# Accumulating Strassen products onto copies in PSUM, with two more weight pairs of the first block pair in Strassen form

## The chip, the cores and the metric

The kernel runs on one core of one Trainium2 chip. The metric is device microseconds (us) of one execution. Five engines take part: PE (TensorE, the matrix products), ACT (ScalarE), DVE (VectorE), POOL (GpSimd) and SP (SyncE, which issues most DMAs). Matrix products land in PSUM, which has eight banks of 128 x 512 float32; ACT and DVE read and write it.

## The reference

```python
# chunked attention: 8 batches, 8 heads, 576 tokens, chunks of 64, head_dim 64
scores = scale * np.matmul(q_c, k_c.transpose(0, 1, 2, 4, 3))
attn = softmax(scores)
x = np.matmul(attn, v_c)          # laid out as 4608 tokens x 512
# a gated layer on it: w_in 512 x 2048, w_out 2048 x 512
h = x @ w_in
g = h * np.clip(h + 3.0, 0.0, 6.0) / 6.0
out = (g @ w_out).astype(np.float32)
```

## The kernel before, in words

**Tiles.** The 4608 tokens are nine blocks of 512. An attention unit such as 21 is half of the heads of block 2. The hidden size of 2048 is 16 tiles of 128, the contraction over 512 is four slices. Every operand of the large products is split into a high and a low float32r part, and `passes` (lines 471 to 475) issues three matmuls of 128x512 for one slice: high by high, high by low, low by high.

**Block 0** is computed plainly: steps `a`, `b` (first product), `c` (second product). **The other eight blocks** go in four pairs, s = 0 to 3. A pair's two blocks and the hidden tiles p and p+8 form a 2x2 problem, for p = 0 to 7, which `first_product` (line 1040) does in Strassen form: seven products `f1` to `f7` in the order `ORDER_A`, each two slices by three matmuls, so 42 matmuls for a p. In plain form a p takes four tiles of four slices by three matmuls, so 48. In the pair s = 0 the first `NPL` = 4 of the p are done plainly, since their weight sums are not made yet; they are made later from weight tiles (`sum_steps`, line 558; the list `LATER`).

**How the seven products are put together.** Before, product 1, 5, 6 and 7 each get a fresh bank. ACT copies product 1 to SBUF (`p1`, line 1090). DVE adds: `u2` = product 6 + `p1`, `u4` = product 5 + `u2`, `s7` = product 7 + `u4`, and after products 3 and 4 `s3` and `s4` (all through the helper at line 1032). Product 2 accumulates onto product 1's bank after `p1`, product 3 onto that of 5 after `u4`, product 4 onto that of 7 after `s7`. Each of the four results goes through `add_relu_gate` (line 902): ACT writes relu into a tile `r` (line 907), DVE multiplies it with the bank into a `wb` tile (line 910). `second_product` (line 1153) has the same form on the eight weight tiles of w_out, in units of two banks e = 0, 1, and sends sums out of line 1165.

**What sets the order.** Every step is added to `Schedule` with an engine, a cost, the steps it comes after and a due time. `order` (line 102) works the latest start of each step back from the due times and lists the steps engine by engine; each engine then runs its list in order, and an engine that waits holds up all that is behind it. PSUM banks are taken in rings through `take`: ring h has two banks, ring o four. The weight sums for the Strassen form go through `whole` (a load of 256 KB by two DMAs at line 575 if the weight tile is in `KEPT`, else DVE adds at 578), `comb` (DVE, lines 583 and 586), `top` (ACT, 591), `less` (DVE, 594) and `send` (DMAs at 599).

The lines on which product 3's wait rests:

```python
j = {2: 1, 3: 5, 4: 7}.get(i, i)
if i == j:
    after += take_bank(i, name, [id_({1: "gate2.", 5: "gate3.", 7: "gate4.", 6: "gate7."}[i])])
else:
    after.append(id_({2: "p1.", 3: "u4.", 4: "s7."}[i]))
```

Of the kernel before, what the change touches and what calls it, by code (L numbers as in the profile page):

```python
# [18 lines left out]
P = 128  # L19
CH = 64  # L20
# [17 lines left out]
ORDER_B = (1, 5, 6, 7, 2, 4, 3)  # L38
# [20 lines left out]
KEPT = [f"a{i}" for i in range(8)] + ["b3", "b7"]  # L59
# [6 lines left out]
AFTER = {7: -14}  # L66
DUE = {'10': 13.5, '11': 15.25, '20': 16.5, '21': 21, '30': 28, '31': 34.25, '40': 37, '41': 37.5}
SUMS = (-8, 3.7, 2, 0.8)
# [5 lines left out]
TURNS = {1: [*range(NPL, NFP), *range(NPL)]}  # L74
# [3 lines left out]


class Schedule:  # L80
# [21 lines left out]
    def order(self):  # L102
# [47 lines left out]
def tile_kernel(ctx: ExitStack, tc: tile.TileContext, qk_in, v_in, weights, out):  # L150
# [85 lines left out]
    class Attention:  # L236
# [116 lines left out]
        def product(self, bank=None, part=(0, 1)):  # L353
            if part[0]:
                po = self.po
            elif bank:
                po = [bank().rearrange("p (a i t) -> p a i t", a=2, t=CH) for _ in HALF]
                self.src = [t.rearrange("p a i t -> p (a i) t") for t in po]
            else:
                t = self.out()  # L360
                po = self.po = [t[:, s].rearrange("p (a i t) -> p a i t", a=2, t=CH) for s in range(2)]
                self.src = t.rearrange("p s (k t) -> p s k t", t=CH)
            for a in part:
                for i in range(NB // 2):
# [29 lines left out]
    class First(Attention):  # L394
# [122 lines left out]
    def store(n, et, ps):  # L517
        if et % 2 == 0:
# [39 lines left out]
    def sum_steps(m, p):  # L558
# [12 lines left out]
        def whole():  # L571
            t["a"] = borrow(4 * (p % 2), F32)[:, :1024].rearrange("p (f t) -> p f t", f=2) if late else sp.tile([P, 2, 512], F32, name="a")
# [15 lines left out]
        def high():  # L588
            t["hl"] = parked[m, p] = borrow(4 * (p % 2) + 1, F32R).rearrange("p (f k l t) -> p f k l t", f=2, k=2, l=2) if late else hp.tile([P, 2, 2, 2, 256], F32R, name="hl")
# [11 lines left out]
        def send_own():  # L601
            for i, row, col in ((1, 0, 0), (2, 0, 1), (4, 1, 1)):
# [6 lines left out]
    GRAIN = [2] * NSUP  # L609
    turns = lambda s: TURNS.get(s, [*range(NFP)])  # L610
    parts = lambda t, n, g: [t[:, k:min(k + g, n)] for k in range(0, n, g)]
    stream = [t for s in range(NSUP) for t in [t for p in turns(s) for h in range(2) for t in parts(stream_a[p, h], 4 - h, GRAIN[s]) if s]
              + [t for i in ORDER_B for h in range(2) for t in parts(stream_b[i, turns(s)[4 * h] // 4], 4, GRAIN[s])]]
# [24 lines left out]
    def next_slot(s, name, until, stream=False):  # L638
# [10 lines left out]
        if len(work.rings[f"slot{k}"]) == 1:  # L649
            before = [f"f4.0.{2 * (k % 4) + 1}" if 2 * (k % 4) >= NPL else f"b{2 * NFT + 2 * k + 1}", *owns(k)]  # L650
# [37 lines left out]
    def first_x_steps():  # L688
# [19 lines left out]
        def high(i):  # L708
            ops[0][i] = w_tile(f"a{HELD[i]}", F32R)
            ACT.copy(out=ops[0][i][:, :, 0], in_=t(i))  # L710

        def lower(i):
            DVE.tensor_tensor(out=ops[0][i][:, :, 1], in0=t(i), in1=ops[0][i][:, :, 0].bitcast(F32), op=ALU.subtract)
# [10 lines left out]
        for i, last in ((5, "x0.s0"), (6, "x0.s1"), (7, "x0.s2"), (4, "x0.s3")):  # L724
            k = HELD[i]
            before = work.take(f"slot{k}", 1, f"x0.{i}h", [f"f{i}.0.{NFP - 1}"])
            assert not before
            work.add(f"x0.{i}h", "ACT", 1.05, [last, f"b{2 * NFT + 2 * k + 1}", *owns(k)], lambda i=i: high(i))
            work.add(f"x0.{i}l", "DVE", 1.22, [f"x0.{i}h"], lambda i=i: lower(i))

    def operand(s, i, ct):
        if s == 0 and i in (1, 2, 3):
            x = xs[{1: (1, 0), 2: (1, 1), 3: (2, 1)}[i]]
            return x[:, 0, ct], x[:, 1, ct]
        x = ops[s][i][:, ct]
# [20 lines left out]
    def attention(u, due, scores=(), less=(), keep=(), bank=None):  # L756
# [10 lines left out]
        if u in ROWS:  # L767
# [4 lines left out]
                  ["v" + u, *(["qk" + after, *[x for _ in HALF for x in work.take(*RINGS[bank], "product" + u, [made[u], *alike.get(u, [])])]] if after else [])]),  # L772
# [52 lines left out]
    PLACES = {"20": ("a", NFT), "21": ("a", NFT + 10), "30": ("f", 0, 4), "31": ("s", 0, 0), "40": ("s", 0, 2), "41": ("s", 0, 4)}  # L825
    AT = {1: (("f", 1, 4), ("f", 1, 7), ("s", 1, 2), ("s", 1, 4)), 2: (("f", 2, 3), ("f", 2, 6), ("s", 2, 1), ("s", 2, 4))}
# [28 lines left out]
    RINGS = {}  # L855
    bank_h, bank_o = lambda: ps_h.tile([P, NT], F32, name="h"), lambda: ps_o.tile([P, NT], F32, name="acc")
    RINGS.update({bank_h: ("h", 2), bank_o: ("o", 4)})
# [72 lines left out]
    for pos, (n, ft) in enumerate(mm):  # L930
        j = n * NFT + ft
        prev = mm[pos - 1][0] * NFT + mm[pos - 1][1]
        first, second, relu, gate, high, lower, sums, send, bank, under = tile_steps(n, ft)
# [3 lines left out]
        before = [] if apart and j % 2 else [f"b{prev}" if pos else None]  # L937
        work.add(f"a{j}", "PE", PART / 3 if apart else PART, [f"{'high' if apart else 'lower'}a{ft // 2}" if n == 0 else None, *before, "keep00" if apart else made[f"{n}0"], *work.take("o" if spare_bank(pos) else "h", 4 if spare_bank(pos) else 2, f"a{j}", [f"gate{j}"])], first, due=at)
# [18 lines left out]
        for et in range(NET):  # L957
# [3 lines left out]
            if j == 0:  # L961
                before += work.take("o", 4, name, [f"copy{et}"])
# [28 lines left out]
    for u in [*[u for u in range(NFP) if u not in AFTER], *range(NFP + NPL, 2 * NFP), *AFTER, *LATER]:  # L991
        m, p = 1 - u // NFP, u % NFP
        whole, combine, high, lower, send, send_own = sum_steps(m, p)
        due = SECOND + AFTER[u] if u in AFTER else STEPS + SUMS[0] + SUMS[1] * (u - 7) if u < NFP else STEPS + SUMS[2] + SUMS[3] * PART * 7 * (p - NPL) if p >= NPL else START[1] + LATE[0] + LATE[1] * p
# [4 lines left out]
        next_ = {0: ["ul0.7.1", "ul0.4.1"], 1: ["ul0.2.1", "ul0.3.1"], 2: [f"send{NFP}"], 3: [f"send{NFP + 1}"]}[p] if late else work.take("hl", 2, f"top{u}", [f"send{u}", *last])  # L999
# [11 lines left out]
    SLOT_OF = (2, 0, 5, 6, 4, 1, 3, 7)  # L1011
    FREED = (3, 5, 7, 2, 6, 4, 1, 0)

    bank = lambda i: ps_h.tile([P, NT], F32, name="h") if i in (6, 3) else ps_o.tile([P, NT], F32, name="acc")
    take_bank = lambda i, name, until: work.take("h", 2, name, until) if i in (6, 3) else work.take("o", 4, name, until)
# [24 lines left out]
    def first_product(s):  # L1040
# [5 lines left out]
        for at, p in enumerate(turns(s) if s else range(NPL, NFP), 0 if s else NPL):  # L1046
            t = {}
            more = lambda r, p=p: left(p + NFP * r) if s == 0 else [f"less{u}s" for u in LATER] if s == 1 and p < 2 else [f"send{u}" for u in LATER] if s == 1 and p < NPL else []
# [3 lines left out]
            for k, i in enumerate(ORDER_A):  # L1052
                name = id_(f"f{i}.")
                j = {2: 1, 3: 5, 4: 7}.get(i, i)
                feed, until = feeds[ceil(4) * (k // 4) + k % 4 // g] if s else (None if i in (1, 2, 4) else f"less{NFP + p}s", [])
                over = s and (k % 4 % g == g - 1 or k == 6)
                after = [before, feed, f"x{s}.{i}l" if s or i in HELD else None]
                if i == j:
                    after += take_bank(i, name, [id_({1: "gate2.", 5: "gate3.", 7: "gate4.", 6: "gate7."}[i])])
                else:  # L1060
                    after.append(id_({2: "p1.", 3: "u4.", 4: "s7."}[i]))

                def product(i=i, j=j, k=k, t=t, over=over, p=p):
                    w = ahead[0][:, k % 4 % g] if s else weight_of(p, i)
                    ps = t[j] if i != j else keep_tile(t, i, lambda: bank(i))
                    for ct in range(2):
                        o = slice(ct * P, ct * P + P)
                        passes(ps, w[:, 0, o], w[:, 1, o], *operand(s, i, ct), i == j and ct == 0, ct == 1, i != j)
# [3 lines left out]
                due = START[s] + PART * (7 * at + k)  # L1072
# [6 lines left out]
                def fresh(key, p=p):  # L1079
                    if s:  # L1080
# [216 lines left out]
```

## Time and profile before

| what | value |
|---|---|
| time, median of 3 runs | 765.35 us (765.1 to 765.86) |
| the profiled execution, span from first to last instruction | 764.3 us |
| what lies around the span, against the median | 1.05 us |
| instructions | 13998 |
| PE busy | 757.2 us, 99% of the span |
| DVE busy | 640.9 us, 84% |
| ACT busy | 451.2 us, 59% |
| DMA | 198.05 MB, 259 GB/s on average |

The page gives no time of the profiled execution other than its span, so a run's time is read as the span and 1.05 us around it. Busy time is summed over instructions; PE's matmuls overlap and their ends are modelled, so how far apart they start says more than how long they are busy. "[0.55 <-DVE u L1032]" behind a row means that the engine was idle for 0.55 us before it and that a DVE instruction of line 1032, which writes `u`, released it.

### The profile page before, as it was taken

The page shows a single profiled execution, that of the slowest core. Times are in us where ns is not written, and L with a number is a line of the kernel's source. Part 1 is how long each engine was busy: PE and PEld are TensorE (multiplying, and loading weights), DVE is VectorE, ACT ScalarE, POOL GpSimd, SP SyncE. Part 2 cuts the span into 40 slices and gives each one's busy share as a digit, 9 for nine tenths or more (in the row PEclk, how much of TensorE's full clock was granted, in tenths as well). Part 3 has the DMA queues.
Part 4 walks back from the last instruction along what each step waited for, and adds up shares of the span by engine and source line. Part 5 has one row for each costly group of instructions (what it writes and reads, how often), then busy time and mean ns, then how long its engine had stood idle before and what let it go on. Part 6 is the DMA issues. An engine that isn't in the chain of part 4 may idle for free.

```text
span 764.3 us, 13998 instructions
## 1 busy us (share of the span) xinstructions
PE 757.2 (99%) x5457; PEld 621.4 (81%) x5457; DVE 640.9 (84%) x805; ACT 451.2 (59%) x884; POOL 69.9 (9%) x74
## 2 busy tenths in 40 slices
PE   8999999999999999999999999999999999999998
PEld 5788788888888888788888888888888888888887
DVE  6989989898999999898999697689996667679751
ACT  6898967675768844356884444557853333355330
POOL 0000000000000010121200103201001123221010
PEclk9999999999999999999999999999999999999999
DMA  9999999959486898986667865757657666565572
GB/s 370 406 361 374 330 354 343 314 206 313 168 288 242 294 389 279 319 267 211 216 241 243 315 229 195 256 195 274 197 195 238 218 211 193 194 207 193 193 242 90
DMA packets 67442, 198.05 MB, mean 259 GB/s; under 512 B 7024, under 2 KB 19568, under 8 KB 63024
## 3 DMA queue, kind: packets, MB, share of 16 engines
q1 hardware_dynamic: 64752, 188.90, 71.9%
q0 software_dynamic: 2480, 8.13, 2.7%
q8 instruction: 43, 0.70, 0.4%
q14 instruction: 23, 0.19, 0.1%
q10 hardware_dynamic: 144, 0.13, 0.1%
HBM read 153.09 MB, written 44.04 MB: 258 GB/s over the span
## 4 chain that ended last, share of the span: by engine, by line
PE 85%; DMA 5%; DVE 5%; ACT 3%; issue 1%; SPq 0%; DVEq 0%; ACTq 0%
PE acc L473 21%; PE acc L474 20%; PE acc L475 20%; PE h L473 7%; PE h L474 7%; PE h L475 7%; DMA wb<-w_in_out 3%; PE two L263 2%; PE h L367 1%; DMA wb<-wa 1%; DMA xd<-qk_in 1%; ACT r L212 1%; ACT e L345 1%; ACT u L208 1%; DVE u L215 1%
## 5 line engine op out<-in xcount | busy, mean ns | idle before, releaser
L473 PE MATMUL acc<-wa,ws 128*128 128x512 f32 (+1 forms) x536 | 208.8, 390 | 0.5 <-DVE u L1032 0.5
L474 PE MATMUL acc<-wa,ws 128*128 128x512 f32 (+1 forms) x536 | 207.8, 388 | 0.0
L475 PE MATMUL acc<-wa,ws 128*128 128x512 f32 (+1 forms) x536 | 207.8, 388 | 0.0
L1140 ACT CAST wa<-wb 128x1024 fp32r<-128x1024 f32 x96 | 100.1, 1053 | 78.2 <-PE acc L475 49.1
L1144 DVE TENSOR_TENSOR wa<-wb,wa 128x1024 fp32r<-128x1024 f32 x96 | 119.0, 1257 | 17.3 <-ACT wa L1140 17.2
L473 PEld LDWEIGHTS acc<-wa,ws 128*128 128x128 f32 x536 | 100.6, 188 | 22.2 <-DVE u L1032 1.3
L475 PEld LDWEIGHTS acc<-wa,ws 128*128 128x128 f32 x536 | 100.6, 188 | 20.7
L474 PEld LDWEIGHTS acc<-wa,ws 128*128 128x128 f32 x536 | 100.7, 188 | 20.2
L907 ACT ACTIVATE r<-acc,half 128x512 f32<-128x512 f32 x90 | 61.8, 688 | 35.6 <-DVE acc L1032 31.2
L907 ACT ACTIVATE r<-h,half 128x512 f32<-128x512 f32 x38 | 26.3, 692 | 86.1 <-DVE h L1032 81.4
L910 DVE SCALAR_TENSOR_TENSOR wb<-r,acc 128x512 f32<-128x512 f32 x90 | 61.1, 681 | 6.1 <-ACT r L907 6.0
L474 PE MATMUL h<-wa,ws 128*128 128x512 f32 (+1 forms) x144 | 55.2, 383 | 0.0
L475 PE MATMUL h<-wa,ws 128*128 128x512 f32 (+1 forms) x144 | 55.2, 383 | 0.0
L473 PE MATMUL h<-wa,ws 128*128 128x512 f32 (+1 forms) x144 | 55.2, 383 | 0.0
L298 ACT ACTIVATE e<-two,m 128x64 f32<-128x64 f32 x160 | 48.4, 333 | 7.8 <-DVE m L292 6.4
L1172 POOL DMA_DIRECT2D out_t<-o x15 | 8.4, 557 | 429.6 <-DVE o L1165 428.5
L1107 POOL TENSOR_TENSOR wb<-wb 128x512 f32<-128x512 f32 x18 | 25.1, 1396 | 174.7 <-DVE wb L910 142.9
L1032 DVE TENSOR_TENSOR u<-h,p 128x512 f32<-128x512 f32 x32 | 21.9, 687 | 22.8 <-PE h L475 21.9
L1032 DVE TENSOR_TENSOR acc<-acc,u 128x512 f32<-128x512 f32 x48 | 33.0, 694 | 5.8 <-PE acc L475 5.8
L298 ACT ACTIVATION_READ_ACCUMULATOR e<-two,m 128x1 f32 x160 | 36.1, 225 | 0.0
L910 DVE SCALAR_TENSOR_TENSOR wb<-r,h 128x512 f32<-128x512 f32 x38 | 25.8, 680 | 10.7 <-ACT r L907 10.7
L473 PE MATMUL acc<-wa,wa 128*128 128x512 f32 x88 | 34.6, 393 | 0.0
(247 smaller groups left out, 1460.5 us busy)
## 6 DMA issues: line engine op xcount, KB each, us to landing
ws<-b SPq DMA_DIRECT2D x84, 512.0 KB, 4.6
ws<-a SPq DMA_DIRECT2D x72, 512.0 KB, 4.6
qk<-qk_in SPq DMA_DIRECT2D x17, 1024.0 KB, 7.6
wa<-b SPq DMA_DIRECT2D x28, 512.0 KB, 5.8
v<-v_in SPq DMA_DIRECT2D x17, 512.0 KB, 5.3
wa<-w_in_out SPq DMA_DIRECT2D x8, 1024.0 KB, 12.0
wb<-w_in_out SPq DMA_DIRECT2D x8, 1024.0 KB, 11.1
a<-wa SPq DMA_DIRECT2D x32, 256.0 KB, 4.8
```

Of the source, the lines that this page charges most:

```text
L263: PE.matmul(self.s[to, a, 2 * i + k, :], lhsT=self.qk[rows, 0, 2 * i + s, o], rhs=self.qk[rows, 1, 2 * i + s, o], start=True, stop=True)
L298: ACT.activation(out=self.flat(self.e)[:, c], in_=self.flat(self.s)[:, c], func=AF.Exp, bias=self.m[:, c:c + 1], scale=SCALE, accum_out=se ...
L473: PE.matmul(ps, lhsT=a_h, rhs=b_h, start=first, stop=False, skip_group_check=more)
L474: PE.matmul(ps, lhsT=a_h, rhs=b_l, start=False, stop=False, skip_group_check=more)
L475: PE.matmul(ps, lhsT=a_l, rhs=b_h, start=False, stop=last, skip_group_check=more)
L907: ACT.activation(out=t["r"], in_=ps(), func=AF.Relu, bias=half, scale=1.0 / 6.0)
L910: work.add("gate" + name, "DVE", 0.69, ["relu" + name, *more], lambda: DVE.scalar_tensor_tensor(out=out(), in0=t["r"], scalar=1.0, in1=ps( ...
L1032: return lambda: DVE.tensor_tensor(out=out(), in0=x(), in1=y(), op=ALU.add)
L1107: work.add(id_("t1."), *on[1:], [id_("gate3."), id_("gate2.")], lambda f=gq, on=on[0]: on.tensor_tensor(out=f(0, 1), in0=f(0, 1), in1=f(0, ...
L1140: ACT.copy(out=g_ops[s, i, pp][:, :, 0], in_=src())
L1144: work.add(low, *(("POOL", 2.5) if on else ("DVE", 1.22)), [high], lambda i=i, pp=pp, src=src, on=POOL if on else DVE: on.tensor_tensor(ou ...
L1172: nc.gpsimd.dma_start(out=out[out_rows, out_cols], in_=sums_at[out_rows.start, out_cols.start])
```

## The change

- `NPL` goes from 4 to 2: the p = 2 and 3 of the pair s = 0 are now in Strassen form as well. Their weight sums (numbers 10 and 11) move from the late list to the early one, `SUM_ORDER`. `KEPT` gains b2 and b6, so sums 4 and 5 are loaded rather than added. Four high/low results are put into weight tiles (`PARKED`).
- The four banks of ring o become two rings of two, y and z, beside ring h. Product 6 accumulates onto an ACT copy of product 1 in PSUM (`p1`, ring z), product 7 onto an ACT copy of product 6's bank (`u2`, ring h), product 5 is copied to SBUF (`p5`). DVE adds only `s7` and `s3`. `ORDER_A` puts product 2 between 6 and 7. The second product of the pairs 0 to 2 has the same form.
- `relu` writes into the gate's tile, and the gate is made in place.
- The attention units 20, 21, 40, 41 and those after them are merged in at other places (`PLACES`, `AT`).
- A table `SHIFTS` adds a number to the latest start of some 120 steps, and `WAIT` 8 us to late due times, ahead of the listing.

```diff
-NPL = 4
+NPL = 2
-HELD = {5: 0, 6: 4, 7: 1, 4: 5}
-ORDER_A = (1, 5, 6, 7, 2, 3, 4)
+HELD = {5: (0,), 6: (5, 6), 7: (4,), 4: (7,)}
+ORDER_A = (1, 5, 6, 2, 7, 3, 4)
...
-KEPT = [f"a{i}" for i in range(8)] + ["b3", "b7"]
+KEPT = [f"a{i}" for i in range(8)] + ["b2", "b3", "b6", "b7"]
...
+SUM_ORDER = (0, 10, 1, 11, 2, 12, 13, 3, 14, 15, 4, 5, 6, 7)
+PARKED = {10: "b2", 11: "b6", 13: "a1", 15: "a2"}
+WAIT = 8.0
+SHIFTS = """
+qk40=-33.0 v40=31.3 exp2_000=-530.0 invert100=10.4 share100=10.1 less101=15.5 share101=-280.6 turned101=-296.9 keep01=-308.3 max10=-11.9 less10=-11.5
...
+        shifts = dict(x.split("=") for x in SHIFTS.split())
+        latest = {n: t + float(shifts.get(n, 0)) for n, t in latest.items()}
...
+    def new_bank(ring):
+
+        return (ps_h if ring == "h" else ps_o).tile([P, NT], F32, name=ring)
...
-        work.add("relu" + name, "ACT", 0.69, [after, *work.take("r", 2, "relu" + name, ["gate" + name])], relu, due=due)
-        work.add("gate" + name, "DVE", 0.69, ["relu" + name, *more], lambda: DVE.scalar_tensor_tensor(
-            out=out(), in0=t["r"], scalar=1.0, in1=ps(), op0=ALU.min, op1=ALU.mult), due=due)
+        work.add("relu" + name, "ACT", 0.69, [after, *more], lambda: ACT.activation(out=out(), in_=ps(), func=AF.Relu, bias=half, scale=1.0 / 6.0), due=due)
+        work.add("gate" + name, "DVE", 0.69, ["relu" + name], lambda: DVE.scalar_tensor_tensor(
+            out=out(), in0=out(), scalar=1.0, in1=ps(), op0=ALU.min, op1=ALU.mult), due=due)
...
+                after = [before, feed, f"x{s}.{i}l" if s or i in HELD else None, f"lay{s}" if i == 1 else id_({5: "lie.", 6: "p1.", 2: "p1.", 7: "u2.", 3: "u2.", 4: "s7."}[i])]
...
+                    fresh = i in (1, 5)
...
+                        passes(t[{2: 1, 3: 6, 4: 7}.get(i, i)], w[:, 0, o], w[:, 1, o], *operand(s, i, ct), fresh and ct == 0, ct == 1, not fresh)
...
+                if i == 1:
+                    work.add(id_("p1."), "ACT", 0.59, [name, id_("lie.")], copy(6, 1), due=due)
+                elif i == 5:
+                    work.add(id_("p5."), "ACT", 0.59, [name, *work.take("p1" if s else "first", 2, id_("p5."), [id_("s7."), id_("s3.")])], copy("p5", 5, beside), due=due)
                 elif i == 6:
+                    work.add(id_("u2."), "ACT", 0.59, [name, *work.take("h", 2, id_("u2."), [id_("gate4.")])], copy(7, 6, lambda: new_bank("h")), due=due)
                 elif i == 7:
-                    work.add(id_("s7."), "DVE", 0.69, [name, id_("u4.")], add(of(6), of(7), of("u4")), due=due)
+                    work.add(id_("s7."), "DVE", 0.69, [name, id_("p5.")], plus(5, 7), due=due)
```

How the lists move, at three places.

ACT, first product of the pair s = 3 (before: lines 1090 and 907; after: 1132 and 954). `h`, `acc`, `y`, `z` are PSUM banks, `p` and `wb` are in SBUF. Before, one p and the next:

```order
L1090 COPY p_6409<-acc 128x512
L907 ACTIVATE r<-h,half 128x512
L907 ACTIVATE r<-acc,half 128x512 x3
L1090 COPY p_6485<-acc 128x512
L907 ACTIVATE r<-h,half 128x512
```

After, one p:

```order
L1132 COPY z<-h 128x512
L1132 COPY p_6268<-y 128x512
L1132 COPY h<-z 128x512
L954 ACTIVATE wb_3627<-h,half 128x512
L954 ACTIVATE wb_3637<-y,half 128x512
L954 ACTIVATE wb_3627<-z,half 128x512
L954 ACTIVATE wb_3637<-h,half 128x512
```

A p has three copies on ACT where it had one, two of them from PSUM to PSUM, and the four relus as before.

DVE, the same place (before: lines 1032 and 910; after: 1135 and 955). Before:

```order
L1032 TENSOR_TENSOR u_6428<-h,p_6409 128x512
L1032 TENSOR_TENSOR u_6430<-acc,u_6428 128x512
L1032 TENSOR_TENSOR h<-acc,u_6430 128x512
L910 SCALAR_TENSOR_TENSOR wb_3698<-r,h 128x512
L910 SCALAR_TENSOR_TENSOR wb_3711<-r,acc 128x512
L1032 TENSOR_TENSOR acc<-acc,u_6428 128x512 x2
```

After:

```order
L955 SCALAR_TENSOR_TENSOR wb_3627<-wb_3627,h 128x512
L1135 TENSOR_TENSOR y<-h,p_6338 128x512
L1135 TENSOR_TENSOR z<-z,p_6338 128x512
L955 SCALAR_TENSOR_TENSOR wb_3637<-wb_3637,y 128x512
L955 SCALAR_TENSOR_TENSOR wb_3627<-wb_3627,z 128x512
```

Five additions of a p become two, `s7` (into y) and `s3` (into z).

DVE, first product of the pair s = 0, where weight sums are made between its steps (`a`, `hl` and, after the change, some `wa` tiles hold the sums; `g` is product 5's copy after the change, and before it `u2` and `u4`). Before:

```order
L586 TENSOR_TENSOR a<-a 128x2x256
L1032 TENSOR_TENSOR g_2016<-h,g_1992 128x512
L583 TENSOR_TENSOR a<-a 128x256
L1032 TENSOR_TENSOR g_2021<-acc,g_2016 128x512
L713 TENSOR_TENSOR wa_1976<-wb_1650,wa_1976 128x2x512
```

After:

```order
L618 TENSOR_TENSOR hl<-a,hl 128x4x256
L610 TENSOR_TENSOR a<-a 128x512
L607 TENSOR_TENSOR a<-a 128x256
L354 STREAM_TRANSPOSE e<-two 128x1024
L1135 TENSOR_TENSOR y<-h,g_2261 128x512
```

In both lists the first sum of a loaded weight tile (line 586, now 610) stands ahead of an addition on which a product waits; behind it now stands `s7`, where `u2` and `u4` stood.

## Rows read from the trace of the kernel before

**Rows 1.** The page, part 1: busy us, share of the span and instructions of each engine.
```profile
PE 757.2 (99%) x5457; PEld 621.4 (81%) x5457; DVE 640.9 (84%) x805; ACT 451.2 (59%) x884; POOL 69.9 (9%) x74
```

**Rows 2.** Timeline of PE: start, us; first of 24 matmuls and the next.
```profile
36.06 0.39 PE L473 MATMUL acc<-g,wb 128*128 128x512 f32 x1
...
41.50 0.39 PE L473 MATMUL acc<-g,wb 128*128 128x512 f32 x1
```

**Rows 3.** Waits of PE: line, waited for, total us, times, longest.
```profile
PE acc L473 <- DVE u L1032: 0.5, 1, 0.5
...
PE two L367 <- ACT e L345: 0.3, 1, 0.3
...
PE acc L473 <- DVE g L1032: 0.2, 1, 0.2
```

**Rows 4.** Timeline, 313 to 322 us: a sum that waited for its load, and PE.
```profile
313.09 0.69 DVE L586 TENSOR_TENSOR wb<-wb 128x512 f32<-128x512 f32 x1 [1.81 <-DMA wb<-wa]
...
320.87 0.39 PE L475 MATMUL acc<-wa,ws 128*128 128x512 f32 x1
...
321.06 0.69 DVE L1032 TENSOR_TENSOR u<-acc,u 128x512 f32<-128x512 f32 x1
...
321.81 0.50 PE L473 MATMUL acc<-wa,ws 128*128 128x512 f32 x1 [0.55 <-DVE u L1032]
...
322.15 0.39 PE L474 MATMUL acc<-wa,ws 128*128 128x512 f32 x1
```

**Rows 5.** The chain of waits in order of time: start us, us, what.
```profile
305.82 7.18 DMA wb<-wa
```

**Rows 6.** Timeline: a product's last matmul and the copy that waits for it.
```profile
184.75 0.39 PE L475 MATMUL acc<-xb,wa 128*128 128x512 f32 x1
...
185.18 0.59 ACT L1090 COPY g<-acc 128x512 f32<-128x512 f32 x1 [0.21 <-PE acc L475]
```

**Rows 7.** Groups by line and shape: count, busy us, mean ns, idle before.
```profile
L1140 ACT CAST wa<-wb 128x1024 fp32r<-128x1024 f32 x96 | 100.1, 1053 | 78.2 <-PE acc L475 49.1 <-PE h L475 15.4 <-DVE wb L1122 3.3
...
L1090 ACT COPY p<-acc 128x512 f32<-128x512 f32 x24 | 14.0, 582 | 5.8 <-PE acc L475 5.8
...
L282 ACT ACTIVATE two<-two 128x1024 f32<-128x1024 f32 x6 | 6.1, 1010 | 0.1
...
L1032 DVE TENSOR_TENSOR acc<-acc,u 128x512 f32<-128x512 f32 x48 | 33.0, 694 | 5.8 <-PE acc L475 5.8
...
L1032 DVE TENSOR_TENSOR u<-h,p 128x512 f32<-128x512 f32 x32 | 21.9, 687 | 22.8 <-PE h L475 21.9 <-issue 0.7
```

**Rows 8.** Timeline: attention unit 21 from its scores to its product.
```profile
117.28 0.50 PE L473 MATMUL h<-xb,wa 128*128 128x512 f32 x1
...
118.07 1.22 DVE L275 TENSOR_REDUCE m<-two 128x16 f32<-128x1024 f32 x1
...
132.29 1.19 ACT L345 COPY e<-two 32x512 f32<-32x512 f32 x2
...
135.19 1.16 PE L367 MATMUL acc<-e,v 64*64 64x64 f32 x64
```

**Rows 9.** Timeline, 149 to 181 us: sums that waited for loads, PE's wait.
```profile
149.19 0.69 DVE L586 TENSOR_TENSOR a<-a 128x512 f32<-128x512 f32 x1 [0.58 <-DMA a<-wb]
...
153.61 0.69 DVE L586 TENSOR_TENSOR a<-a 128x512 f32<-128x512 f32 x1 [0.18 <-DMA a<-wa]
...
177.05 0.69 DVE L586 TENSOR_TENSOR a<-a 128x512 f32<-128x512 f32 x1 [1.06 <-DMA a<-wa]
...
180.18 0.39 PE L475 MATMUL acc<-xc,wa 128*128 128x512 f32 x1
...
180.73 0.50 PE L473 MATMUL acc<-xd,hl 128*128 128x512 f32 x1 [0.16 <-DVE g L1032]
...
181.07 0.40 PE L474 MATMUL acc<-xd,hl 128*128 128x512 f32 x1
```

**Rows 10.** Windows, 26 to 115 us: PE, PEld, DVE, ACT, POOL busy, clock, DMA share, GB/s.
```profile
26.00:115.00 89.00, 88.72 (x638) 72.41 (x631) 82.05 (x102) 75.92 (x123) 0.00 (x0) 1.00 0.99 363
```

More of the change, by code (lines that the diff above doesn't have):

```diff
@@ L73 @@
 LATE = (-8, 8)
-TURNS = {1: [*range(NPL, NFP), *range(NPL)]}
+TURNS = {1: [*range(4, NFP), *range(4)]}
 STORE = 3.0
@@ L649, in next_slot @@
         if len(work.rings[f"slot{k}"]) == 1:
-            before = [f"f4.0.{2 * (k % 4) + 1}" if 2 * (k % 4) >= NPL else f"b{2 * NFT + 2 * k + 1}", *owns(k)]
+            before = [f"f4.0.{next((u % NFP for u in PARKED if PARKED[u] == f'a{k}'), 2 * (k % 4) + 1)}", *owns(k)]
         return k, before
@@ L706, in op, with room, high, lower @@
             return lambda: engine.tensor_tensor(out=t(i), in0=x(), in1=y(), op=kind)
[L708 to L713, printed above, removed]
+        def room(i):
+            unused = [(w[f"a{k}"][:, :, 0, :256], w[f"a{k}"][:, :, 1, :256]) for k in HELD[i]]
+            return unused + [tuple(rp.tile([P, NT], F32R, name="r") for _ in range(2))] * (2 - len(unused))
+        like = lambda x, to: x.rearrange("p (f t) -> p f t", f=2) if len(to.shape) == 3 else x
+        def high(i, k):
+            if not k:
+                ops[0][i] = room(i)
+            to = ops[0][i][k][0]
+            ACT.copy(out=to, in_=like(t(i)[:, k], to))
+        def lower(i, k):
+            of, to = ops[0][i][k]
+            DVE.tensor_tensor(out=to, in0=like(t(i)[:, k], to), in1=of.bitcast(F32), op=ALU.subtract)
+        def both(i, f):
+            whole = ops[0][i] = w_tile(f"a{HELD[i][0]}", F32R) if f is high else ops[0][i]
+            if f is high:
+                ACT.copy(out=whole[:, :, 0], in_=t(i))
+            else:
+                DVE.tensor_tensor(out=whole[:, :, 1], in0=t(i), in1=whole[:, :, 0].bitcast(F32), op=ALU.subtract)
         x = lambda n, dp, k: lambda: half_of(n, dp, k)
@@ L724, in first_x_steps @@
         for i, last in ((5, "x0.s0"), (6, "x0.s1"), (7, "x0.s2"), (4, "x0.s3")):
[L725 to L729, printed above, removed]
+            last = [last, *[x for k in HELD[i] for x in (owns(k) if i in (5, 7) else [])], *([f"b{2 * NFT + 2 * HELD[i][0] + 1}"] if i in (5, 7) else [f"b{NFT - 1}"]),
+                    *(["glow15"] if i == 4 else [])]
+            for k in HELD[i]:
+                assert not work.take(f"slot{k}", 1, f"x0.{i}h", [f"f{i}.0.{NFP - 1}"])
+            if i in (5, 7):
+                work.add(f"x0.{i}h", "ACT", 1.05, last, lambda i=i: both(i, high))
+                work.add(f"x0.{i}l", "DVE", 1.22, [f"x0.{i}h"], lambda i=i: both(i, lower))
+                continue
+            work.add(f"x0.{i}h", "ACT", 0.62, last, lambda i=i: high(i, 0))
+            work.add(f"x0.{i}h1", "ACT", 0.62, [f"x0.{i}h"], lambda i=i: high(i, 1))
+            work.add(f"x0.{i}l0", "DVE", 0.70, [f"x0.{i}h"], lambda i=i: lower(i, 0))
+            work.add(f"x0.{i}l", "DVE", 0.70, [f"x0.{i}l0", f"x0.{i}h1"], lambda i=i: lower(i, 1))
     def operand(s, i, ct):
@@ L1047, in first_product @@
             t = {}
[L1048 removed]
+            more = lambda r, p=p: left(p + NFP * r) if s == 0 else [f"less{u}s" for u in LATER] if s == 1 and p < 2 else [f"send{u}" for u in LATER] if s == 1 and p < 4 else []
             gq = lambda r, c, p=p: gate_of(r, c, p)
@@ L1087, in first_product, with beside, copy, plus @@
-                ring = "" if s else "first"
+                def beside(p=p):
+                    if s:
+                        return tp.tile([P, NT], F32, name="p1")
+                    if p % 2 == 0:
+                        laid[0] = pair_of(1, F32)
+                    return laid[0][:, p % 2]
+                def copy(to, of, fresh=None, t=t):
+                    return lambda: ACT.copy(out=keep_tile(t, to, fresh) if fresh else t[to], in_=t[of])
+                def plus(to, of, t=t):
+                    return lambda: DVE.tensor_tensor(out=t[to], in0=t[of], in1=t["p5"], op=ALU.add)
@@ L1164, in f @@
                     part = slice(NT // n * k, NT // n * (k + 1))
+                    if y is None:
+                        ACT.copy(out=o[:, part], in_=x()[:, part])
+                        continue
                     DVE.tensor_tensor(out=o[:, part], in0=(x()[k] if n > 1 else x())[:, part], in1=y()[:, part], op=ALU.add)
```

181 lines of the change are left out of this document (98 added, 83 removed).

## The prediction, made before the changed kernel was run

> **What bounds the kernel now.** I read the page first: PE is busy for 757.2 of 764.3 us, DVE for 84%, ACT for 59% [rows 1]. Busy time of PE is modelled, so the next view is the timeline: 24 matmuls of 128x512 start within 41.50 - 36.06 = 5.44 us, 0.2267 us each [rows 2]. The same pitch holds from the first weight tiles to the end, except at the small matmuls of attention units and where PE waits. So I listed who PE waits for: eight waits, and past the first 30 us only three, 0.5, 0.3 and 0.2 us [rows 3]. A wait costs more than its idle time, because the first matmul behind it starts its successor late: 321.81 to 322.15 is 0.34 us, not 0.227, so 0.11 us for a restart [rows 4]. PE's own stream is thus the bound. DVE and ACT matter only where PE waits for one of their steps.
>
> The Trainium skill (Perfetto Trace Analysis, section "Identifying the Most-Contended Engine") says that the busy share of matmuls is a bad measure of how near TensorE is to its limit, and that the busy share of weight loads is better. By that rule the 81% of PEld would leave a fifth of PE's time free and matmuls taken out could be worth nothing; the trace agrees with its first half, for 0.39 us of "busy" stands on a pitch of 0.2267, and not with the second, since that pitch never shrinks.
>
> **The change, part by part.**
>
> *Fewer matmuls.* Two p go from 48 matmuls to 42, so 12 x 0.2267 = 2.72 us less on PE, all on the path. **-2.72.**
>
> *The longest wait goes.* PE's 0.55 us at 321.8 was product 3 of a p in pair 1, held by the DVE addition `u4` [rows 4]. Behind it stands a load of a late weight sum, 7.18 us long in the chain of waits [rows 5], for which the sum at 313.09 held DVE for 1.81 us [rows 4]. From 320.87 to 322.15 are 1.28 us where two pitches are 0.45: the place cost 0.83. The change drops `u4`, and of four late sums it keeps two, 8 and 9; the one that was last is now made some 200 us earlier. **-0.83**, bounds -0.83 and 0 (if another step takes its place).
>
> *Three new short covers for each p.* Product 6 now waits for a copy of product 1, product 7 for a copy of product 6, product 4 for `s7` of product 7; each has one product of 6 x 0.2267 = 1.36 us in between. Before, product 2 came four products behind 1 and product 4 three behind 7. The cover is counted from the rows. A product's last matmul starts at 184.75, so its slot ends at 184.98; the copy on ACT starts at 185.18, 0.20 later [rows 6]; a copy takes 0.58 us and an addition 0.69 [rows 7]; from the end of a DVE step, 321.06 + 0.69 = 321.75, to PE's start at 321.81 are 0.06 us [rows 4]. A copy needs 0.84 and leaves 0.52 of the 1.36; `s7` needs 0.95 and leaves 0.41. No row shows a plain copy from PSUM to PSUM. The nearest is an activation in place in a PSUM tile, 1.01 us for 1024 elements [rows 7]: half of it is 0.51, the whole 1.01, and even 1.01 + 0.26 is under 1.36. I take 0.58, the copy of the same size. So the 90 handoffs (30 p by three) are covered if ACT or DVE is free when the product ends. **0**; the other bound is a cast of 1.05 us [rows 7] begun just before, which makes a copy up to 0.53 late, 0.64 with the restart, at perhaps four places: +2.6. What favours 0 is that the lister lets an engine wait for a step that is soon ready and much more urgent, and that in pair 3 nothing but copies and relus stands in ACT's list.
>
> *Work moved from DVE to ACT.* DVE loses some 107 instructions of 128x512, at 0.69 us 74 us; ACT gains 86 copies, 50 us. Neither is the bound (84% and 59%), so this by itself is **0**.
>
> *Attention unit 21 comes sooner.* In the old trace its scores end by 117.28 and its product starts at 135.19, 78 matmuls or 17.7 us later. Its own chain runs from the maximum at 118.07 to the last swap, which ends at 132.29 + 1.19 = 133.48: 15.4 us [rows 8]. In the changed PE list 66 matmuls stand between, 15.0 us. The chain shared ACT and DVE with other steps, so its least time is shorter, but not by much: bounds 0 and 15.4 + 0.3 - 15.0 = 0.7. I take **+0.4**.
>
> *Loaded weight sums.* In the old list six sums are loaded in the pair-0 stretch, three of which held DVE for their load (0.58, 0.18 and 1.06 us), and one reached PE: 180.18 to 181.07 is 0.89 us for two pitches, 0.43 lost [rows 9]. In the changed SP list ten are, four of them (4 to 7) right through pair 0's Strassen steps, and a held DVE now delays `s7`, with its 0.41 us of cover. I take three that reach PE instead of one: **+0.86**. Bounds: none, -0.43, and all ten, +3.9.
>
> *Start.* Two more weight tiles are written out, 1 MB in a stretch in which the DMA engines are busy for 0.99 of the time at 363 GB/s [rows 10]: 2.9 us of transfers. What hides it is that later weight tiles are loaded ahead of their use; without that cover it costs up to 2.9. I take **0**. The order of the first attention steps on DVE changes too: 0, bounds half a us on either side.
>
> **Sum.** -2.72 - 0.83 + 0.4 + 0.86 = -2.29 us against the profiled execution: a span of 764.3 - 2.3 = 762.0, and with the 1.05 us around it 763.1. The same 1.05 ties the span to the median of 765.35, so that the forecast is 765.35 - 2.29 = **763.1 us**.
>
> **The rivals.**
>
> *Loads in the way.* All ten loaded sums hold DVE and reach PE, +3.9 in place of +0.86. For it: the list is built with a fixed landing time, and three of six were late already. Against: five of six found PE covered. 765.35 - 2.72 - 0.83 + 0.4 + 3.9 = 766.1. A milder form, five or six of ten, gives 764.4: no change that can be told.
>
> *Late copies, slower than before.* ACT's list in pairs 0 to 2 is mixed with exps, casts and swaps of attention units, and 22 of the 30 p lie there, 66 handoffs. If a late one loses on average half of 0.53 and 0.11, 0.38 us, then ten late ones, one in seven, cost 3.8 and give 766.9, just slower; from there it decides. For it: a cast takes twice the cover. Against: the covers above, and ACT's 59% with only 50 us more.
>
> *The freed slots are not on the path.* If PE were held by something else, 12 matmuls fewer would give nothing: 765.35 - 0.83 + 1.26 = 765.8. The Trainium skill's rule on matmul busy time would point here; the constant pitch speaks against it.
>
> **How the numbers follow.** About 0.2%, 1.5 us, is what a measurement of this kernel can tell from no change, so faster is below 763.8 and slower above 766.9. The forecast and what lies below it, 0.62. Loads in the way, 0.20, of which 0.18 within 0.2% and 0.02, together with late copies, above. Late copies, 0.14: 0.06 mild, 0.08 slower. Freed slots not on the path, 0.04. So faster 0.62, same 0.28, slower 0.10. The range goes from 761.7 (-2.72 - 0.83 with the loads and unit 21 costing nothing net) to 766.1 (all loads); outside it some 0.05 below and 0.12 above.
>
> **What would show it.** In the new profile the waits of PE past 30 us should be few: one for unit 21's swap near 130 us, two or three behind `s7` or a copy between 100 and 210 us with a load behind them, none near 320. The ACT copies from PSUM to PSUM should read 0.58 us, the pitch 0.2267, DVE near 570 us busy and ACT near 500. Ten or more short waits for line 1132, spread over pairs 1 and 2, would show late copies; waits for DMA on line 610 with PE waits behind them, the loads. A span that stays at 764 with no more waits than before would make the first term wrong.

## The result and the profile after

The changed kernel takes **769.89 us** (median of 5 runs, 769.1 to 771.13) against 765.35 us for the kernel before in runs beside it (764.92 to 766.17): a ratio of 1.0054 (the two medians alone give 1.0059), 95% interval 1.0042 to 1.0066. It is slower by half a per cent, where 763.1 us was forecast and 766.1 was the end of the range. The profiled execution took 769.67 us.

From its page, parts 1 and 3 (busy time by engine; DMA queues with packets, MB and share of 16 engines' span), which answer to [rows 1]:

```profile
span 767.7 us, 13864 instructions
...
PE 756.4 (99%) x5443; PEld 620.6 (81%) x5445; DVE 575.0 (75%) x699; ACT 500.5 (65%) x972; POOL 68.9 (9%) x74
...
q8 instruction: 43, 0.70, 0.4%
```

DVE and ACT moved as forecast, to 575 and 500 us. PE's busy time hardly fell. Part of that is a stretch at a lower clock: in experiment 1 below, which has none there, PE is busy for 755.2 us. The waits of PE that lie past 19 us, beside [rows 3]:

```profile
PE s L485 <- issue: 2.3, 1, 2.3
PE z L494 <- ACT z L1132: 1.7, 2, 1.3
...
PE z L494 <- DMA wa<-b: 0.3, 1, 0.3
PE z L386 <- DVE wb L955: 0.3, 1, 0.3
```

The wait for `u4` at 321 us is gone. At the top stands one of a kind that the old list didn't have: "issue" is time in which PE waited for nothing that the profile shows. Here it is in the timeline of PE (start us, us, line, operation, in brackets the idle time ahead):

```profile
18.43 0.46 PE L282 MATMUL two<-qk 64*64 64x64 f32 x16
18.89 0.69 PE L485 MATMUL s<-g,g 64*64 64x64 f32 x32
19.41 0.65 PE L485 MATMUL s<-xc,g 64*64 64x64 f32 x28
22.41 0.34 PE L485 MATMUL s<-xc,g 64*64 64x64 f32 x4 [2.35 <-issue]
22.68 2.93 PE L509 MATMUL h<-xa,wa 128*128 128x512 f32 x6
25.40 0.91 PE L509 MATMUL h<-xd,wa 128*128 128x512 f32 x2
...
28.91 1.07 PE L509 MATMUL h<-xd,wa 128*128 128x512 f32 x4
29.82 0.39 PE L494 MATMUL h<-xa,wa 128*128 128x512 f32 x1
```

The same stretch before:

```profile
18.77 0.67 PE L466 MATMUL s<-xc,g 64*64 64x64 f32 x32
19.95 1.63 PE L488 MATMUL h<-xa,wa 128*128 128x512 f32 x6 [0.52 <-DVE wa L221]
...
25.80 0.46 PE L263 MATMUL two<-qk 64*64 64x64 f32 x16
26.19 0.50 PE L473 MATMUL h<-xa,wa 128*128 128x512 f32 x1
```

In the changed kernel PE stops in the middle of one product of unit 01, four matmuls from its end, on the same two tiles as the 28 ahead (matmuls are counted here as the trace records them). Before, the last 16 matmuls of unit 10's scores (`two<-qk`) stood behind the first two hidden tiles; now all four parts stand ahead. And once PE goes on, it is slow. The changed kernel by windows (length, busy time of PE, PEld, DVE, ACT and POOL, then TensorE's granted clock, DMA share, GB/s):

```profile
20.00:22.00 2.00, 0.06 (x3) 0.00 (x0) 1.97 (x3) 1.01 (x2) 0.00 (x0) 1.00 0.99 406
22.00:24.00 2.00, 1.59 (x7) 1.32 (x7) 0.64 (x2) 1.22 (x2) 0.00 (x0) 0.65 1.02 414
24.00:26.00 2.00, 2.00 (x6) 1.52 (x6) 1.58 (x3) 1.50 (x2) 0.00 (x0) 0.50 1.00 311
26.00:28.00 2.00, 2.00 (x10) 1.62 (x9) 0.43 (x1) 0.26 (x1) 0.00 (x0) 0.99 0.93 356
```

Having stood still for 2.35 us, PE is granted 0.50 of its clock, the 1.2 GHz level, from 22.6 to 26.0 us. Tiles 0 and 1 take 29.82 - 22.68 = 7.14 us; before, 25.80 - 19.95 = 5.85. The first matmul of tile 2 comes 3.63 us later than before.

**Where the span went.** 767.7 - 764.3 = +3.4 us, from the two traces:

| piece | us |
|---|---|
| up to tile 2 (29.82 against 26.19) | +3.63 |
| 12 matmuls fewer, at 0.2267 | -2.72 |
| later waits and restarts of PE, 4.09 against 1.61 | +2.48 |

The later 4.09, each with its restart, are: product 6 of a p at 188.30, 1.53; of another at 292.24, 0.75; unit 31's product at 213.63, 0.61; a weight tile of the second product at 227.14, 0.55; unit 21's product, 0.35; a bank at 130.23, 0.30. The 1.61 before are the wait for `u4`, 0.83, the one at 180.73, 0.43, and unit 20's product at 81 us, 0.35. The largest of the later ones, in all engines' timeline (rows of PE's other matmuls left out):

```profile
184.81 0.69 DVE L610 TENSOR_TENSOR a<-a 128x512 f32<-128x512 f32 x1 [1.87 <-DMA a<-wb]
...
185.42 0.69 DVE L1135 TENSOR_TENSOR z<-z,g 128x512 f32<-128x512 f32 x1
...
186.14 0.69 ACT L954 ACTIVATE wb<-z,half 128x512 f32<-128x512 f32 x1 [1.90 <-DVE z L1135]
...
186.65 0.39 PE L496 MATMUL y<-wa,hl 128*128 128x512 f32 x1
186.73 1.03 ACT L615 CAST wa<-a 128x1024 fp32r<-128x1024 f32 x1
...
187.66 0.59 ACT L1132 COPY z<-h 128x512 f32<-128x512 f32 x1
...
188.30 0.50 PE L494 MATMUL z<-wa,hl 128*128 128x512 f32 x1 [1.26 <-ACT z L1132]
```

Read upwards: PE waits for the copy of product 1 (line 1132); the copy stands behind the cast of weight sum 15, the cast behind a relu, the relu behind `s3`, and `s3` behind the addition for sum 4, for whose load DVE was held 1.87 us. Sum 4 is one of those that the change loads.

### The profile page after: what moved, and what is told of

Its sections match the earlier page's. It is cut to its first block, busy times and chain, and to the rows that moved or that the text cites. A ratio compares the mean times of both kernels' runs of the same rounds, so it can differ in the third digit from the quotient of the medians.

```text
span 767.7 us, 13864 instructions
## 1 busy us (share of the span) xinstructions
PE 756.4 (99%) x5443; PEld 620.6 (81%) x5445; DVE 575.0 (75%) x699; ACT 500.5 (65%) x972; POOL 68.9 (9%) x74
## 4 chain that ended last, share of the span: by engine, by line
PE 88%; DMA 6%; DVE 3%; issue 1%; SPq 1%; ACT 1%; DVEq 0%; ACTq 0%
PE h L494 12%; PE h L496 12%; PE h L495 12%; PE z L494 9%; PE z L496 9%; PE z L495 9%; PE y L494 7%; PE y L496 7%; PE y L495 7%; DMA wa<-b 2%; PE two L282 2%; DMA a<-wb 1%; DMA qk<-qk_in 1%; PE h L509 1%; DMA a<-hl 1%
## 5 line engine op out<-in xcount | busy, mean ns | idle before, releaser
L494 PE MATMUL h<-wa,ws 128*128 128x512 f32 (+1 forms) x288 | 112.1, 389 | 0.0
L495 PE MATMUL h<-wa,ws 128*128 128x512 f32 (+1 forms) x288 | 111.3, 386 | 0.0
L496 PE MATMUL h<-wa,ws 128*128 128x512 f32 (+1 forms) x288 | 111.3, 386 | 0.0
L955 DVE SCALAR_TENSOR_TENSOR wb<-wb,h 128x512 f32<-128x512 f32 x64 | 43.9, 686 | 72.0 <-ACT wb L954 71.6
L494 PE MATMUL z<-wa,ws 128*128 128x512 f32 (+1 forms) x232 | 89.5, 386 | 0.5 <-ACT z L1132 0.5
L495 PE MATMUL z<-wa,ws 128*128 128x512 f32 (+1 forms) x232 | 89.4, 385 | 0.0
L496 PE MATMUL z<-wa,ws 128*128 128x512 f32 (+1 forms) x232 | 89.4, 385 | 0.0
L494 PEld LDWEIGHTS h<-wa,ws 128*128 128x128 f32 x288 | 54.1, 188 | 11.6 <-DVE y L1135 0.5
L496 PEld LDWEIGHTS h<-wa,ws 128*128 128x128 f32 x288 | 54.1, 188 | 10.9
L495 PEld LDWEIGHTS h<-wa,ws 128*128 128x128 f32 x288 | 54.1, 188 | 10.9 <-DVE wa L698 0.2
L494 PE MATMUL y<-wa,ws 128*128 128x512 f32 x160 | 62.5, 390 | 0.0
L496 PE MATMUL y<-wa,ws 128*128 128x512 f32 x160 | 62.3, 389 | 0.0
L495 PE MATMUL y<-wa,ws 128*128 128x512 f32 x160 | 62.3, 389 | 0.0
L1229 POOL DMA_DIRECT2D out_t<-o x27 | 14.8, 549 | 491.2 <-ACT o L1220 388.4
L954 ACT ACTIVATE wb<-h,half 128x512 f32<-128x512 f32 x64 | 44.1, 690 | 21.4 <-PE h L496 20.0
L494 PEld LDWEIGHTS z<-wa,ws 128*128 128x128 f32 x232 | 43.6, 188 | 9.6 <-ACT z L1132 0.9
L496 PEld LDWEIGHTS z<-wa,ws 128*128 128x128 f32 x232 | 43.6, 188 | 8.7
L495 PEld LDWEIGHTS z<-wa,ws 128*128 128x128 f32 x232 | 43.6, 188 | 8.7
```

Of the source, the lines that this page charges most:

```text
L495: PE.matmul(ps, lhsT=a_h, rhs=b_l, start=False, stop=False, skip_group_check=more)
L496: PE.matmul(ps, lhsT=a_l, rhs=b_h, start=False, stop=last, skip_group_check=more)
L954: work.add("relu" + name, "ACT", 0.69, [after, *more], lambda: ACT.activation(out=out(), in_=ps(), func=AF.Relu, bias=half, scale=1.0 / 6. ...
L955: work.add("gate" + name, "DVE", 0.69, ["relu" + name], lambda: DVE.scalar_tensor_tensor(out=out(), in0=out(), scalar=1.0, in1=ps(), op0=A ...
L1229: nc.gpsimd.dma_start(out=out[out_rows, out_cols], in_=sums_at[out_rows.start, out_cols.start])
```

## The experiments

The theory: PE ran out of instructions. I take the 43 packets of 16 KB on queue q8 above for PE's: 10,888 records on PE and PEld by 43 are some 253 for each, and the packets begin that far apart in PE's list on average, from the first to the last. The second packet begins at 19.89 us by its record, and PE goes on 2.52 us later. The Trainium skill (Runtime: NRT & Kernel Launch, section "Instruction fetch mechanics") also has refills in blocks of 16 KiB, and calls their cost mostly hidden; by that rule the start would have cost next to nothing. The trace agrees for the other packets, with no issue wait over 0.2 us, and disagrees for this one, with 2.35 us of standing PE. The rival is that the start hangs on the first weight tile and on loads, whatever PE's order.

Each kernel below takes the finished list and moves steps in it, `>x` to behind x, `<x` to ahead of it:

```diff
     listed = work.order()
+    move = {'scores10': '<a2'}
+    for step, to in move.items():
+        step = listed.pop([name for name, _ in listed].index(step))
+        listed.insert([name for name, _ in listed].index(to.lstrip("<>")) + (to[0] == ">"), step)
```

**1. The scores behind again** (the diff above, in the changed kernel: `scores10` is the last part of unit 10's scores, `a2` the first step of tile 2).

> The changed kernel with one step moved on PE alone: the last of the four parts of unit 10's scores (16 matmuls in the trace) goes from ahead of the first two hidden tiles to behind them, as in the kernel before. First theory (PE ran out of instructions): the changed kernel's PE reaches its 349th matmul at 20.06 us, and the next instructions are there only at 22.41; with 16 matmuls fewer ahead of that place PE meets it in the middle of the first two tiles, after 22.4 us or a little before, so the issue wait of 2.35 us shrinks to under 0.3 us, the 3.4 us at the 1.2 GHz level go with it, and the time falls by 3.3 to 3.7 us, to 766.2 to 766.6 us. Rival (the start is bound by the first weight tile on DVE and by loads): the wait only changes its name, the first matmul of tile 2 stays at 29.8 us and the time at 769.9 us, within 0.5.

766.03 us (764.21 to 767.46, 11 runs), beside 766.26 for the kernel before; ratio 0.9998, 0.9990 to 1.0007. PE's timeline:

```profile
19.69 0.67 PE L485 MATMUL s<-xc,g 64*64 64x64 f32 x32
20.88 1.62 PE L509 MATMUL h<-xa,wa 128*128 128x512 f32 x6 [0.52 <-DVE wa L240]
...
26.51 0.46 PE L282 MATMUL two<-qk 64*64 64x64 f32 x16
26.91 0.50 PE L494 MATMUL h<-xa,wa 128*128 128x512 f32 x1
```

No issue wait, no lower clock, the two tiles in 5.63 us, and 3.9 us off the median, a little more than the theory's 3.3 to 3.7. The rival's 769.9 is out. The start is 2.91 us of it in the two traces (29.82 against 26.91); the rest lies behind tile 2, in waits that change from run to run (experiment 7). And with its start mended the changed kernel is as fast as the one before, not 2.29 us faster as the prediction's sum had it.

**2. The converse in the kernel before**: `move = {'scores10': '<a0'}`.

> The converse in the kernel before: the same last part of unit 10's scores goes ahead of the first two hidden tiles, nothing else moves. First theory (PE ran out of instructions): the 349th matmul is now one of these scores and is reached at about 19.7 us instead of 22.7; the refill of instructions began at 19.27 in the kernel before and, if it again takes the 2.5 us that it took in the changed kernel, is there at 21.8, so PE shows an issue wait of about 2 us, then some microseconds at the 1.2 GHz level, and the time rises by 2.5 to 3.7 us, to 767.9 to 769.1 us. Rival (the start is bound by the first weight tile and by loads): PE waited for that weight tile until 19.95 anyway, so the 16 matmuls fill idle time and the time is 765.4 us or up to 0.4 less.

769.29 us (768.68 to 771.43, 5 runs) against 766.26; ratio 1.0040, 1.0026 to 1.0054: 3.0 us for moving 16 matmuls past idle time, within the theory's 2.5 to 3.7. The profile is that of the slowest of the five runs, 771.43 us. Its timeline, and then its windows:

```profile
19.36 0.40 PE L263 MATMUL two<-qk 64*64 64x64 f32 x12
22.59 0.48 PE L263 MATMUL two<-qk 64*64 64x64 f32 x4 [2.83 <-issue]
23.00 2.93 PE L488 MATMUL h<-xa,wa 128*128 128x512 f32 x6
...
31.14 0.39 PE L473 MATMUL h<-xa,wa 128*128 128x512 f32 x1
```

```profile
24.00:26.00 2.00, 2.00 (x6) 1.59 (x5) 0.64 (x1) 0.00 (x0) 0.00 (x0) 0.50 1.13 375
26.00:28.00 2.00, 2.00 (x6) 1.51 (x6) 0.00 (x0) 0.00 (x0) 0.00 (x0) 0.50 0.87 336
28.00:30.00 2.00, 2.00 (x9) 1.63 (x8) 0.21 (x1) 0.93 (x2) 0.00 (x0) 0.87 1.02 430
```

Counted through PE's list as the trace shows it (each of the scores' f32 matmuls twice), this stop and that of the changed kernel both come behind the 349th matmul, here within the scores, there within a product. A wait on data has no reason to keep its place in the count. The second packet began at 20.20, and PE went on 2.39 us later; in experiments 3 and 7 it went on 2.33 us after it. Before, and in experiment 1, the 349th is the 12th matmul of tiles 0 and 1, passed at about 22.8 and 23.5, 0.7 to 1.2 us after the packet (begun at 19.27 and 20.28) had its 2.3 to 2.5 us.

**3. The addition for sum 4 later** (in the changed kernel): `move = {'comb4': '>s3.0.5'}`.

> The changed kernel with one step moved on DVE alone: the addition that waits for the load of weight sum 4 (1.87 us of held DVE at 184.8 us) goes behind the addition to product 3's bank that stood right behind it. Theory (a held DVE delays relu, relu the cast, the cast the copy of product 1, and product 6 waits 1.26 us for it): that wait goes or falls under 0.2 us, and since PE is the bound from there on, the time falls by 1.1 to 1.4 us, to 768.5 to 768.8 us. Rival (the wait moves on to the next copy or to a later load): PE waits the same 1.2 us within the next 30 us and the time stays at 769.9 us.

769.17 us (768.25 to 769.56, 5 runs), 0.7 to 0.9 less than the changed kernel's 769.89 and, below, 770.02. Its waits of PE:

```profile
PE s L485 <- issue: 2.2, 1, 2.2
...
PE z L494 <- ACT z L1132: 0.9, 1, 0.9
...
PE z L494 <- DMA wa<-b: 0.6, 1, 0.6
...
PE h L494 <- ACT h L1132: 0.4, 1, 0.4
```

The wait of 1.26 at 188 us is gone, so its cause is shown; but a copy soon after it is now 0.4 late, and the waits at 225 and 290 us are 0.25 and 0.45 longer; the one at 213 us is not in this trace, where the load ahead of it held DVE for 0.42 us instead of 1.26. The time is between the two theories.

**4. No table**: `SHIFTS = """"""`.

> The changed kernel with the table SHIFTS left empty: products, rings, sums and the added 8 us stay, only the listing differs. In its PE list the last part of unit 10's scores stands behind the first two hidden tiles, as in the kernel before. First theory (PE ran out of instructions, and the table put the scores there): no issue wait at 20 us and no stretch at the 1.2 GHz level, 3.6 us less at the start, and what waits the table was meant to spare comes back later, unknown, 0 to 4 us: 766 to 770 us. Rival (the loss lies in the new form of the products and its handoffs, not in the listing): waits behind copies at the same places as in the changed kernel and a time of 769.5 us or more.

776.59 us (774.63 to 778.15, 4 runs): above the theory's 766 to 770, which had the later waits as unknown, and within the rival's 769.5 or more. Tile 2 begins at 26.80, with no issue wait, so the table did put the scores ahead. But PE waits far more later, and not behind copies (line 1120), as the rival had it, but mostly for gates (943), an operand (742) and a load:

```profile
PE h L482 <- DVE wb L943: 1.9, 1, 1.9
PE h L483 <- DVE wa L742: 1.8, 1, 1.8
PE z L482 <- DMA wa<-b: 1.1, 1, 1.1
PE z L374 <- DVE wb L943: 1.1, 1, 1.1
PE h L482 <- ACT h L1120: 0.9, 1, 0.9
```

Against experiment 1, with the same start, the table spares 776.59 - 766.03 = 10.6 us.

**5. The start wholly as before**: `move = {'scores0_10': '>product000', 'scores1_10': '>product00', 'scores10': '<a2'}`.

> The changed kernel with three steps moved on PE alone: the last part of unit 10's scores behind the first two hidden tiles, as in the first experiment, and the first and second part behind the two half products of unit 00, as in the kernel before, so that PE doesn't wait 0.5 to 1 us for unit 10's load with work behind it that is ready. Theory (the start is a chain from the load of unit 00 to the first weight tile, which the scores only fill): the first matmul of tile 2 comes at 26.2 us as in the kernel before, not at 26.9 as in the first experiment, and the time is 0.3 to 0.7 us under that experiment's 766.0, 765.3 to 765.7 us. Rival (PE waits for the weight tile on DVE anyway, so what stands ahead doesn't matter once the instructions are there): 766.0 us, within 0.3.

765.60 us (764.51 to 767.75, 11 runs), beside 765.94; tile 2 begins at 26.46. The gain of 0.4 over experiment 1 is within the theory's 0.3 to 0.7, but the kernel before is 0.3 lower in these runs as well, so that nothing clear of the scatter is left: not settled.

**6. Late steps moved as well**: beside the three of experiment 5,

```diff
+    'comb2b': '>gate24', 'top2': '>up21', 'comb4': '>s3.0.5', 'top15': '>p1.0.6', 'comb7': '>s3.0.7',
+    'comb7c': '>gate3.0.7', 'comb7b': '>gate3.0.7', 'less6s': '>gate3.0.7', 'x1.2h': '>p1.1.4'
```

> The kernel of the run before this one with nine more steps moved on DVE and ACT alone, none on PE: the loaded additions of sums 4 and 7 and two short additions go behind the step of a Strassen p that stood right behind them, and three casts (of sums 2 and 15 and of an operand of pair 1) go behind the copy or swap that PE waits for. Theory (each microsecond that PE waits for a copy, a gate or a swap is on the path, and these casts and loaded additions in front of them are why it waits): the waits at 127, 184 and 211 us and the late product of unit 21 go, 0.4 + 1.2 + 0.6 + 0.35 us in the first experiment's trace, together with the one near 290, so the time is 2.0 to 2.8 us under the run before this one, about 763.2 us. Rival (late copies: a cast moved back makes the next copy or the next feed late, as sum 4 did when it was moved alone): half or less of it, 764.3 to 765.5 us, with new waits for line 1132 or for a weight sum's DMA within 30 us of the old places.

764.71 us (763.51 to 766.25, 11 runs) against 765.94; ratio 0.9984, 0.9975 to 0.9993: faster than both kernels, by 0.16% than the one before. That is 0.9 us under experiment 5, less than half of the theory's 2.0 to 2.8 and within the rival's range. The new wait, 0.57 us, is not for a copy or a load, as the rival had it, but for an operand whose cast was moved:

```profile
PE h L495 <- DVE wa L698: 0.6, 1, 0.6
PE h L494 <- DVE wb L955: 0.4, 1, 0.4
```

**7. The changed kernel again**, unchanged.

> The changed kernel itself once more, beside the next run and the kernel before on one chip, since its 769.89 us and the 766.03 of the first experiment come from two sets of runs 0.9 us apart in the kernel before. The start as the traces show it (first matmul of tile 2 at 29.82 against 26.91 us) gives 2.9 us between the two; the medians give 3.9. Theory (the rest is scatter of the later waits from run to run): 769 to 770 us, an issue wait of 2.2 to 2.5 us at 20 us again, and waits behind copies and loads past 30 us that add up to another number than the 3.7 us of the first trace, between 2 and 4. Rival (the moved step also changed something later): the later waits add up to the same 3.7 us within 0.2.

770.02 us (766.47 to 771.64, 6 runs) against 766.05; ratio 1.0047, 1.0029 to 1.0065. The issue wait is there again (2.37 us, behind the same matmul). The wait for the copy at 188 us is 1.83 now instead of 1.26, since sum 4's load held DVE for 2.44, and the clock falls behind this one as well:

```profile
188.00:190.00 2.00, 1.37 (x5) 1.09 (x6) 2.00 (x4) 2.00 (x4) 0.00 (x0) 0.84 0.75 303
190.00:192.00 2.00, 2.00 (x6) 1.56 (x5) 2.00 (x4) 1.12 (x3) 0.00 (x0) 0.50 0.74 249
```

From tile 2 to the last matmul PE takes 735.72 us here, 734.38 in the first trace and 733.29 in experiment 1, with the same PE list. So the later waits do scatter with the loads: they come to some 1.3 us more than the 4.09 of the first trace, which is out of the rival's 0.2, but also above the 2 to 4 that the theory gave. One run of the six took 766.47 us, 0.4 over the kernel before, with a mean granted clock of 1.000. It was not profiled, so whether PE stopped in it is not known.

This trace has a second issue wait, eight matmuls from the end of a unit's scores:

```profile
365.81 0.34 PE L282 MATMUL two<-qk 64*64 64x64 f32 x8 [0.71 <-issue]
```

In experiment 3 PE stops at the same place for 0.17 us. Both end 2.43 us after a packet on q8 began, at 363.38 and 361.76. In the first trace that packet began at 362.02, and PE passed the place at 364.70 without a stop. So the place in the list and the time of the packet go together here too, far from the start.

**8. The moves sorted**: those of experiment 6 without `x1.2h`, `top2` behind `relu17`, `less2s` behind `gate25`.

> The kernel with its start as before and the late steps moved, less one move and with two changed: the cast of pair 1's operand stays where the change has it (moved back it made its own product wait 0.57 us at 288), the cast of sum 2 goes behind the two relus as well and its subtraction behind the gate that freed a bank 0.42 us late at 131.9. Theory (each of these is on the path): 0.4 to 0.9 us under the 764.7 us of that kernel, 763.8 to 764.3 us, against a kernel before at 766.0. Rival (what is left is the scatter of loads from run to run, not these steps): 764.7 us, within 0.4.

765.13 us (763.91 to 766.63, 11 runs) against 766.05; ratio 0.9991, 0.9982 to 1.0000. The two waits named are gone from its trace, yet the median is 0.42 us above that of experiment 6, where the theory gave 0.4 to 0.9 less. That is the rival's answer, 0.02 outside its 0.4: what is left there can't be told from scatter.

## Why the prediction was wrong

**The step that failed is "Start".** It read the 1 MB more of stores, at up to 2.9 us, and the order of the first steps on DVE, with half a microsecond either way, and took 0 for both; its rows for this stretch begin at 26 us. It did not look at PE's own list there, in which 16 matmuls change places. They were free by every wait of the old trace, as PE stood 0.52 us for a weight tile. But with them PE came to the 349th matmul ahead of its instructions: +3.63 us in the trace, 2.91 of which go when they move back, and 3.9 off the median. The stores, which stay in experiments 1 and 5, leave tile 2 only 0.72 and 0.27 us later than before.

**Fewer matmuls: right.** The pitch held. In experiment 6 PE goes from tile 2 to its last matmul in 732.81 us against 734.66. Of the 2.72 us 1.85 show; the gaps between large matmuls add up to 0.38 us more than before, and the units' matmuls with the gaps behind them take 0.49 more, 0.42 of it the wait for a bank that experiment 8 takes up. In experiment 8 it is 731.85, 2.81 less, but in the fastest of its runs and with other waits of the old list gone too.

**The longest wait: right, -0.83.** Nothing waits near 321 us.

**Unit 21: right.** +0.4 forecast; its product and the scores behind it take 0.35 us longer than those of the other units. Unit 20's product, 0.35 too long before, no longer is, which the prediction did not count.

**Loaded sums: mis-sized.** Three of the ten held DVE (0.95, 1.87 and 1.26 us; a hold of 3.19 us at 276 us is of a late sum) and two reached PE, not three; but they cost 1.53 + 0.61 = 2.14 us instead of 1.29. The price of 0.43 each came from a load that reached PE through one addition. At 188 us it went through an addition, a relu and a cast before the copy.

**Short covers: 0 was wrong, the bound was right.** The copies take 0.57 to 0.62 us, as taken. But a cast in front can make one late, as the bound of +2.6 had it (timeline of the changed kernel, pair 1):

```profile
290.64 1.06 ACT L695 CAST wa<-xa 128x1024 fp32r<-128x1024 f32 x1
...
291.59 0.60 ACT L1132 COPY z<-h 128x512 f32<-128x512 f32 x1
...
292.24 0.50 PE L494 MATMUL z<-wa,ws 128*128 128x512 f32 x1 [0.49 <-ACT z L1132]
```

This cost 0.75 us with the late start behind it; a bank and a weight tile add 0.85.

**The rivals.** "Late copies" had the right sign and, at 188 and 292 us, the right mechanism, but gave 766.9; "loads in the way" is the same row at 184.81. Neither could reach 769.9, and the range ended at 766.1 because no case had the start in it, not even the 2.9 us for the stores. What lies around the span was mis-sized as well: runs of the kernel before are 1.7 to 1.9 us longer than their spans, not 1.05, so the profile shown was one of about 766.1 us. Of the 6.8 us between forecast and result the start is 3.63, the later waits 2.05 (2.48 where the terms above gave 0.43), and what lies around the span, with the profiled run against the median, the remaining 1.1. Two small sums of the prediction are off without bearing on this: 765.35 - 2.72 - 0.83 is 761.8, not 761.7, and the milder form's 764.4 holds for six loads, where five give 763.9.

## What to carry to other kernels

An engine's own instructions arrive too. Where many small instructions come early, count them up to the place where the engine would next be refilled, on the engine that has the most of them, before moving even "free" work ahead of it. And price a held engine by the whole chain behind it, not by the one step after it: here an addition held for 1.87 us became 1.53 us on PE through a relu, a cast and a copy. A longer wait can cost the clock as well.

## What the runs showed of the hardware that I had not expected

- PE stood for 2.2 to 2.8 us in four profiles, those of the changed kernel and of experiments 2, 3 and 7, each time behind the 349th matmul. In experiment 7 there is a shorter stop of the kind, 0.71 us, within a unit's scores at 365.81 us. What sets when a packet begins stays open: with the same PE order up to there, the second began at 19.27 us before and at 20.20 in experiment 2.
- With each stop at 20 us, and behind the 1.83 us at 188 us in experiment 7, the granted clock fell to 0.50, the 1.2 GHz level, for some microseconds, longest in experiment 2, from 21.7 to 28.5 us; there it fell while PE still stood. Behind the 1.26 us of the first trace it did not, nor behind 1.91 us at 157.7 us in experiment 4. So the length of a wait alone doesn't tell whether the clock falls.
